# Two transformer layers on one core: the split of a later group's raw weights comes one call of the background work behind their load

## The chip, the cores and the metric

The kernel runs on one core of a Trainium2 chip, as one launch. The metric is the time of that launch on the device in microseconds (us); smaller is better.

## What is computed

The input x is 2048 rows of 512 numbers. Two blocks, an attention A and a gated MLP B, are applied twice with the same weights: x = x + A(norm(x)), x = x + B(norm(x)), and once more. The reference, cut to what matters here:

```
def _A_ref(x, wqkv, wo):
    ...  # 32 heads of 16; phi(t) = where(t > 0, t + 1, exp(t)) + 1e-6
    kv = jnp.einsum("bhsd,bhse->bhde", pk, v)
    ...
    return (num / den) @ wo

def _B_ref(x, w1, w3, w2):          # x 2048x512, w1 and w3 512x1792, w2 1792x512
    gate = jnp.einsum("bsd,df->bsf", x, w1)
    up = jnp.einsum("bsd,df->bsf", x, w3)
    h = _silu(gate) * up
    return jnp.einsum("bsf,fd->bsd", h, w2)

x = A_x
x = x + _A_ref(_layernorm(x), A_wqkv, A_wo)
x = x + _B_ref(_layernorm(x), B_w1, B_w3, B_w2)
x = x + _A_ref(_layernorm(x), A_wqkv, A_wo)
x = x + _B_ref(_layernorm(x), B_w1, B_w3, B_w2)
```

## The kernel before, in words

**Numbers in two parts.** Every float32 operand of a matmul is split into a float16 high part and a float16 rest. `split_late` does it: ScalarE writes the high part at once (L445), and VectorE's rest (L447) is kept in a list, `owed`, and issued when `settle()` is called. `w2` is split by `split` (L412 and L413).

**The MLP.** Its inner width of 1792 is cut into seven groups of 256 columns (numbers 0 to 6), and the 2048 rows into four chunks. In layer 0 the groups come in three sets, (0,1,2), (3,4) and (5,6); a *pass* is one set with one chunk, so there are 4 x 3 + 4 x 2 + 4 x 2 = 28 turns of one group with one chunk. Within a turn, `mlp_group` makes the products in seven parts (a Strassen-like scheme, P1 to P7, twelve matmuls each, L523) into PSUM banks called ba, bb and bc. ScalarE copies a bank out or applies the silu (L1341, L1296), VectorE adds and multiplies (L1344, L1297), four sums (L1312 to L1315, on VectorE or GpSimd) and one more split (L1300 on ScalarE, L1302 on VectorE) make the hidden values, and `mlp_out` (L1388, or L1408 in the plain form) multiplies them by w2 into banks called po. L1437 to L1458 add the result to x.

**The weights.** SBUF holds four slots for split w1/w3 groups. Groups 0 to 2 are prepared during the attention. For groups 4, 3, 5 and 6, in this order, `background` does it during the MLP: `load_raw(g)` issues eight transfers (L547) of 128 KB each into one staging area, the first four for w1 and the last four for w3; `w13_group` splits for w1 one part (128x2x128) and two parts (128x2x256), then the same for w3, makes four sums (L573 to L579) and splits those (128x2x512). `w2_group` follows with two transfers (L778), its splits and sums (L808). It uses the same staging area, half of it for one group, the other half for the next. A load therefore waits for the last reader of its half.

**Who decides the order.** `background` is a generator. After each turn the kernel calls `steps(more, budget)`, with a budget from the table `HOOKS` (0 to 8 in layer 0), under `later(back)`, which gives what is issued a later place in priority:

```
def steps(generator, budget):
    while budget > 0:
        settle()
        step = next(generator, budget)
        budget -= step
```

So a `yield 1` takes one unit and the same call goes on; a yield of more than is left ends the call. Work that a turn needs and that isn't there yet is forced by `ready_for`, step by step. What is issued this way isn't the final order: in the MLP a scheduler of the tile framework places the instructions on each engine by priority and by its own estimate of when they can run. Each engine then executes its list strictly in that order, and an instruction that waits holds up what stands behind it. All DMAs of this kernel are issued from SyncE's queue (SP), in its list's order.

Of the kernel before, what the change touches and what calls it, by code (L numbers as in the profile page):

```python
# [88 lines left out]
def kernel(  # L89
# [21 lines left out]
    def view(at, dtype, *dims):  # L111
        size = 4 if dtype == F32 else 2
        n = size
        for d in dims:
            n *= d
        ap = arena[:, at // 4 : (at + n) // 4]
        if dtype != F32:
            ap = ap.bitcast(dtype)
        if len(dims) > 1:
            names = "abcdefg"[: len(dims)]  # L120
            ap = ap.rearrange(
                f"p ({' '.join(names)}) -> p {' '.join(names)}",
                **{n: d for n, d in zip(names[1:], dims[1:])},
            )
        return ap
# [313 lines left out]
    def settle():  # L439
        while owed:  # L440
            owed.pop(0)()
# [98 lines left out]
    def load_raw(g):  # L540

        dst = view(AT_RAW, F32, 2, 2, 2, 2, P)
        for w, name in enumerate(("w1", "w3")):
            for c in range(2):
                for h in range(2):
                    at = h * (F // 2) + g * P
                    nc.sync.dma_start(dst[:, w, :, c, h], w_rows[name][:, c, :, at : at + P])  # L547

    def w13_group(g, dst):

        if g > 2:
            raw = view(AT_RAW, F32, 2, 2, 4, P)
            quads = [raw[:, :, :, i] for i in range(4)]
            rows = [(w, raw[:, w, :, 2:4], ((0, raw[:, w]),)) for w in range(2)]
        else:
            cols = [slice(h * (F // 2) + g * P, h * (F // 2) + g * P + P) for h in range(2)]
            quads = [st_w13[:, :, c, :, cols[h]] for c in range(2) for h in range(2)]
            both = [
                [
                    st_w13[:, w, c].rearrange("p k (h n) -> p k h n", h=2)[:, :, :, cols[0]]  # L560
                    for c in range(2)
                ]
                for w in range(2)
            ]
            rows = [(w, both[w][1], ((0, both[w][0]), (2, both[w][1]))) for w in range(2)]
        a11, a21, a12, a22 = quads
        scale = [info[n][2] for n in ("w1", "w3")]
        for w, pair, _ in rows:
            split_late(dst[:, w, 0, :, 0], dst[:, w, 1, :, 0], a11[:, w], scale[w])
            yield heavy[0]  # L570
            split_late(dst[:, w, 0, :, 1:3], dst[:, w, 1, :, 1:3], pair, scale[w])
            yield heavy[0]
        engine_of("w13", g).tensor_tensor(a22, a21, a22, OP.add)  # L573
        yield 1
        engine_of("w13", g).tensor_tensor(a21, a11, a21, OP.subtract)
        yield 1
        engine_of("w13", g).tensor_tensor(a11, a22, a11, OP.subtract)
        yield 1
        engine_of("w13", g).tensor_tensor(a12, a12, a11, OP.subtract)  # L579
        yield 1  # L580
        for w, _, parts in rows:
            for i, src in parts:
                n = src.shape[2]
                to = [dst[:, w, part, :, 3 + i : 3 + i + n] for part in range(2)]
                split_late(to[0], to[1], src, scale[w])
                yield heavy[0] * n / 2
# [167 lines left out]
    def store(what, g, src):  # L754
        to = {"w13": w13_d, "w2": w2_d}[what]
        with in_order("SP"):
            nc.sync.dma_start(to[:, g], src)
# [23 lines left out]
    def w2_group(g):  # L781


        raw = w2_raw(g)
        dst, scale = w2_s[g], info["w2"][2]
        yield 1
        split(dst[:, 0, 0], dst[:, 1, 0], raw[:, 0], scale)
        yield 1
        split(dst[:, 0, 1:3], dst[:, 1, 1:3], raw[:, 2:4], scale)
        yield 1  # L790
        later_plain = any(g in gs and plain_run(1, 4 * i + c) for i, gs in enumerate(SETS[1]) for c in range(NC))
        if later_plain or g in w2_a21 and state["plain"]:

            to = w2_a21.get(g, dst[:, :, 6])
            split(to[:, 0], to[:, 1], raw[:, 1], scale)
            if later_plain:
                with in_order("SP"):
                    nc.sync.dma_start(a21_d[:, g], to)
            have.add(("plain", g))
            yield 1  # L800
        a11, a21, a12, a22 = (raw[:, i] for i in range(4))
        for to, a, b, op in (
            (a22, a21, a22, OP.add),
            (a21, a11, a21, OP.subtract),
            (a11, a22, a11, OP.subtract),
            (a12, a12, a11, OP.subtract),
        ):
            engine_of("w2", g).tensor_tensor(to, a, b, op)  # L808
        yield 1
        split(dst[:, 0, 3:], dst[:, 1, 3:], raw, scale)  # L810
        yield 2
        have.add(("w2", g))

    def background(first):

        for tasks in first[::-1]:
            yield from tasks.rest()
        a, b, c = SETS[0]
        for g in a:
            yield from w2_group(g)  # L820
            store("w2", g, view(AT_W2 + SLOT2[g] * GROUP2, F16, GROUP2 // 2))
        late = view(AT_W + 3 * GROUP, F16, 2, 2, 2, 7, P)
        for g in b[::-1]:
            load_raw(g)
            if g == b[-1]:
                for i in a:
                    store("w13", i, view(AT_W + i * GROUP, F16, GROUP // 2))
            yield 1
            yield from w13_group(g, late)
            if g == b[-1]:  # L830
                store("w13", g, view(AT_W + 3 * GROUP, F16, GROUP // 2))
            settle()
            have.add(("w13", g))
            while state["plain"]:
                yield 100
            yield from w2_group(g)
        while state["set"] < 1:
            yield 100
        for g in c:
            load_raw(g)  # L840
            yield 1
            yield from w13_group(g, w13[g])
            settle()
            have.add(("w13", g))
            yield from w2_group(g)
# [628 lines left out]

    def mlp(layer, prep):
        more = background(prep) if layer == 0 else iter(())

        def ready_for(what, g):
# [271 lines left out]
```

## Time and profile before

| | us |
|---|---|
| median of 3 runs | 1174.78 |
| lowest and highest of them | 1173.83, 1175.29 |
| time of the profiled execution | 1172.7 |
| its span, first to last instruction of the trace | 1170.9 |
| TensorE busy in that span | 1147.1 |

The span is what the trace shows of the profiled execution; 1.8 us of its time lie around it. A matmul counts as busy from its start to its modelled end. In rows of the trace, "idle before" is the time that the engine stood still ahead of a row, and the name behind the arrow is what ended that.

### The profile page before, as it was taken

How to read it: one execution, taken by the hardware profiler on the slowest of the kernel's cores; microseconds unless marked ns; L12 is line 12 of the kernel's file. 1: busy time of each engine (PE TensorE's matmuls, PEld its weight loads, DVE VectorE, ACT ScalarE, POOL GpSimd, SP SyncE). 2: the span in 40 equal slices, each digit the busy share in tenths (PEclk: the TensorE clock that was granted, in tenths of full speed). 3: DMA queues.
4: the chain of work that ended last, by engine and by line, in shares of the span. 5: the costliest groups of instructions: out<-in, count | busy, mean ns of one | idle time of the engine just before them, and what ended most of it. 6: DMA issues, size and time to landing. Idle time of an engine off the chain costs nothing.

```text
span 1170.9 us, 21807 instructions
## 1 busy us (share of the span) xinstructions
PE 1147.1 (98%) x8862; PEld 863.5 (74%) x8862; DVE 832.0 (71%) x1401; ACT 638.3 (55%) x1078; POOL 402.8 (34%) x472
## 2 busy tenths in 40 slices
PE   8999998999999999999999999998999999999998
PEld 3445444788888888888864454477888888888887
DVE  6798889977977897778674568757856675656533
ACT  6677787856544554444456644766444344443422
POOL 4343588321000222113368715771252110303120
PEclk9999999999999999999999999999999999999999
DMA  9977565979632221112217425654351351111011
GB/s 279 323 235 233 122 172 119 279 257 278 155 129 100 83 81 64 64 64 73 73 41 209 122 84 116 130 144 125 86 140 64 127 189 48 50 67 37 1 37 37
DMA packets 163396, 147.43 MB, mean 126 GB/s; under 512 B 129632, under 2 KB 138976, under 8 KB 158688
## 3 DMA queue, kind: packets, MB, share of 16 engines
q1 hardware_dynamic: 163296, 146.04, 43.2%
q8 instruction: 69, 1.13, 0.4%
q14 instruction: 31, 0.25, 0.1%
HBM read 72.48 MB, written 42.07 MB: 98 GB/s over the span
## 4 chain that ended last, share of the span: by engine, by line
PE 73%; DVE 8%; DMA 6%; ACT 5%; POOL 4%; issue 2%; SPq 1%; POOLq 0%; DVEq 0%; ACTq 0%
PE bb L523 19%; PE po L1388 16%; PE bc L523 10%; PE pk L523 6%; PE gt L523 6%; PE pq L523 5%; PE po L523 5%; PE ba L523 4%; DMA arena<-arena 3%; DMA arena<-in_B_w_dram 3%; PE po L1408 2%; POOL arena L1283 1%; DVE arena L447 1%; DVE arena L1283 1%; DVE arena L1437 1%
## 5 line engine op out<-in xcount | busy, mean ns | idle before, releaser
L523 PEld LDWEIGHTS <-arena 128*128 128x128 f16 x6360 | 618.3, 98 | 251.3 <-issue 11.6
L523 PE MATMUL bb<-arena 128*128 128x256 f16 x2688 | 330.6, 273 | 4.8 <-DMA arena<-arena 2.3
L1388 PE MATMUL po<-arena 128*128 128x256 f16 x1932 | 234.8, 273 | 6.2 <-ACT arena L1300 3.2
L1388 PEld LDWEIGHTS <-arena 128*128 128x128 f16 x1932 | 188.3, 98 | 30.7 <-ACT arena L1300 5.0
L1341 ACT ACTIVATE arena<-bb 128x512 f32<-128x512 f32 x196 | 114.9, 588 | 132.7 <-PE bb L523 99.3
L523 PE MATMUL bc<-arena 128*128 128x256 f16 x1344 | 165.9, 273 | 0.3 <-DVE arena L1344 0.2
L1302 DVE TENSOR_TENSOR arena<-arena 128x512 f16<-128x512 f32 (+1 forms) x90 | 104.4, 1160 | 81.1 <-ACT arena L1300 80.9
L1300 ACT ACTIVATE arena<-arena 128x512 f16<-128x512 f32 x112 | 99.8, 891 | 104.9 <-DVE arena L1297 47.2
L1296 ACT ACTIVATE arena<-arena,scalars 128x512 f32<-128x512 f32 x112 | 74.7, 667 | 120.9 <-DVE arena L1344 119.9
L1297 DVE SCALAR_TENSOR_TENSOR arena<-arena,scalars 128x512 f32<-128x512 f32 x112 | 86.0, 768 | 50.8 <-ACT arena L1296 50.7
L1344 DVE TENSOR_TENSOR arena<-arena,bc 128x512 f32<-128x512 f32 x112 | 76.4, 682 | 57.7 <-ACT arena L1341 42.3
L1302 POOL TENSOR_TENSOR arena<-arena 128x512 f16<-128x512 f32 x22 | 25.5, 1157 | 230.9 <-ACT arena L1300 206.8
L1457 POOL TENSOR_TENSOR arena<-arena 128x512 f32<-128x512 f32 x25 | 35.7, 1428 | 195.7 <-DVE arena L1437 186.1
L1437 DVE SCALAR_TENSOR_TENSOR arena<-po,scalars,arena 128x256 f32<-128x256 f32 (+1 forms) x170 | 91.9, 584 | 6.5 <-PE po L1388 6.2
L523 PE MATMUL po<-arena 128*128 128x512 f16 x384 | 87.8, 379 | 2.1 <-DMA arena<-arena 2.0
L523 PE MATMUL ba<-arena 128*128 128x256 f16 x672 | 88.7, 274 | 0.0
L523 PE MATMUL gt<-arena 128*128 128x512 f16 x384 | 87.6, 379 | 0.6 <-ACT arena L953 0.3
L523 PE MATMUL pk<-arena 128*128 128x512 f16 x384 | 87.7, 379 | 0.0
L523 PE MATMUL pq<-arena 128*128 128x512 f16 x384 | 87.6, 379 | 0.1
L500 ACT ACTIVATE arena<-arena,nb_all,rs_all 128x512 f32<-128x512 f32 x64 | 50.2, 806 | 23.9 <-POOL nb_all L497 21.0
L1408 PE MATMUL po<-arena 128*128 128x256 f16 x480 | 57.0, 273 | 1.8 <-ACT arena L1300 1.8
L447 DVE SCALAR_TENSOR_TENSOR arena<-arena,scalars 128x512 f16<-128x512 f32 (+2 forms) x60 | 50.1, 856 | 7.9 <-ACT arena L445 6.5
(163 smaller groups left out, 1265.2 us busy)
## 6 DMA issues: line engine op xcount, KB each, us to landing
arena<-xb_d SPq DMA_DIRECT2D x12, 1792.0 KB, 6.8
xb_d<-arena SPq DMA_DIRECT2D x8, 1792.0 KB, 6.5
xt_d<-arena SPq DMA_DIRECT2D x32, 256.0 KB, 2.8
arena<-xt_d SPq DMA_DIRECT2D x32, 256.0 KB, 3.0
arena<-in_B_w_dram SPq DMA_DIRECT2D x8, 896.0 KB, 6.5
arena<-in_B_w_dram SPq DMA_DIRECT2D x28, 256.0 KB, 4.1
w_d<-arena SPq DMA_DIRECT2D x4, 1792.0 KB, 10.3
arena<-w_d SPq DMA_DIRECT2D x4, 1792.0 KB, 6.9
```

What stands on the lines that cost most here:

```text
L447: lambda: nc.vector.scalar_tensor_tensor(lo, src, scale, hi, OP.mult, OP.subtract)
L500: nc.scalar.activation(dst, x_sb[:, t, :], AF.Identity, scale=rs_all[:, t : t + 1], bias=nb_all[:, t : t + 1],)
L523: nc.tensor.matmul(dst, lhs(a, k), rhs(b, k), start=first and k == 0 and i == 0, stop=last and k == n - 1 and i == len(PASSES) - 1, skip_g ...
L1296: nc.scalar.activation(t, gate, AF.Silu, scale=info["u1"])
L1297: nc.vector.scalar_tensor_tensor(t, up, info["hid"], t, OP.mult, OP.mult)
L1300: nc.scalar.activation(hs[:, 0, lo:hi], t[:, lo:hi], AF.Copy)
L1302: engine.tensor_tensor(hs[:, 1, lo:hi], t[:, lo:hi], hs[:, 0, lo:hi], OP.subtract)
L1341: nc.scalar.activation(dst, bank_, AF.Copy)
L1344: nc.vector.tensor_tensor(dst, dst, bank_, OP.add)
L1388: nc.tensor.matmul(po[:, i * HALF : (i + 1) * HALF], hs[:, a, qx, cs], w2[:, b, qw, :], start=g == ends[0] and i + a + b == 0, stop=g == e ...
L1408: nc.tensor.matmul(acc[n][:, half * HALF : (half + 1) * HALF], hs[:, a, qx, cs], w2_a21[g][:, b] if (i, half) == (0, 1) else w2[:, b, i + ...
L1437: nc.vector.scalar_tensor_tensor(dst, src, cb, to, OP.mult, OP.add)
```

## The change

In `background`, the step behind `load_raw(g)` gives back 9 instead of 1, at both places (groups 4 and 3, and groups 5 and 6). Since no budget is above 8, the call in which a load is issued always ends there, and the first split of that group comes in a later call.

```
             if g == b[-1]:
                 for i in a:
                     store("w13", i, view(AT_W + i * GROUP, F16, GROUP // 2))
-            yield 1
+            yield 9
             yield from w13_group(g, late)
...
         for g in c:
             load_raw(g)
-            yield 1
+            yield 9
             yield from w13_group(g, w13[g])
             settle()
             have.add(("w13", g))
```

What the calls issue moves for three groups: group 4's first three splits from the call behind the fifth turn to the one behind the sixth; group 5's first four splits and its sums from the call behind turn 13 to those behind turns 15 and 16; and group 6's whole load from the call behind turn 20 into the forced steps ahead of its own first use, turn 22. (Group 3's load already ended its call.) Most of that vanishes in the scheduler: but for numbers in buffer names, the lists of all engines are the same up to the place where group 6 is loaded, and again from about 60 us later to the end, and GpSimd's list is the same throughout. No instruction is added or taken away.

On SyncE (all DMAs; L547 group 6's raw w1 and w3, L778 group 5's raw w2, L1462 the rows of the next chunk), at the place where group 6 is loaded, one piece of the difference:

```order
 L1462 DMA arena<-xb_d 128x7168
 L766 DMA arena<-w_d 128x7168
-L547 DMA arena<-in_B_w_dram 128x2x128 x3
-L778 DMA arena<-in_B_w_dram 128x512
-L1462 DMA arena<-xb_d 128x7168
-L778 DMA arena<-in_B_w_dram 128x512
+L547 DMA arena<-in_B_w_dram 128x2x128 x4
+L1462 DMA arena<-xb_d 128x7168
+L778 DMA arena<-in_B_w_dram 128x512 x2
+L547 DMA arena<-in_B_w_dram 128x2x128 x3
+L1462 DMA arena<-xb_d 128x7168
 L547 DMA arena<-in_B_w_dram 128x2x128
```

The fourth w1 transfer of group 6 stood behind two w2 transfers and a load of rows; now it follows the third at once. Three of the four w3 transfers now stand ahead of the next load of rows.

On ScalarE at the same place in the program, before (the second row is the split of group 6's first w1 part, L445):

```order
L1296 ACTIVATE arena<-arena,scalars 128x512
L445 ACTIVATE arena<-arena,scalars 128x2x128
L1296 ACTIVATE arena<-bb,scalars 128x256
L1300 ACTIVATE arena<-arena 128x512
L1341 ACTIVATE arena<-bb 128x512
L1296 ACTIVATE arena<-arena,scalars 128x256
L1341 ACTIVATE arena<-bb 128x512
L1300 ACTIVATE arena<-arena 128x1280
L445 ACTIVATE arena<-arena,scalars 128x2x256
```

And with the change:

```order
L1296 ACTIVATE arena<-arena,scalars 128x512
L445 ACTIVATE arena<-arena,scalars 128x2x128
L1296 ACTIVATE arena<-bb,scalars 128x256
L445 ACTIVATE arena<-arena,scalars 128x2x256
L1300 ACTIVATE arena<-arena 128x512
L1341 ACTIVATE arena<-bb 128x512
L1296 ACTIVATE arena<-arena,scalars 128x256
L1341 ACTIVATE arena<-bb 128x512
L1300 ACTIVATE arena<-arena 128x1280
```

The split of the other two w1 parts (128x2x256), which reads the third and fourth transfer, has moved ahead of five instructions of the current turn. Its rest on VectorE (L447) moves with it, ahead of that turn's L1302, L1344 and L1297. Some 30 us on, ScalarE's split of the first w3 part (128x2x128) moves the same way, ahead of the L1296 (128x256), the L1341 and the L1300 (128x1280) that stood in front of it.

On TensorE, at the matmuls that read what that L1300 writes (po, L1388; bb_3950 belongs to the turn in hand, bb_4087 to the next), before:

```order
L523 MATMUL bc_3951<-arena_66 128x256
L1388 LDWEIGHTS arena_66
L1388 MATMUL po0_3877<-arena_66 128x256
L1388 LDWEIGHTS arena_66
L1388 MATMUL po0_3877<-arena_66 128x256
L523 LDWEIGHTS arena_66
L523 MATMUL bb_3950<-arena_66 128x256
```

And with the change:

```order
L523 MATMUL bc_3951<-arena_66 128x256
L1388 LDWEIGHTS arena_66
L1388 MATMUL po0_3877<-arena_66 128x256
L1388 LDWEIGHTS arena_66
L1388 MATMUL po0_3877<-arena_66 128x256
L523 LDWEIGHTS arena_66
L523 MATMUL bb_4087<-arena_66 128x256
```

The two po matmuls keep their place. Behind them, the twelve matmuls of the turn in hand and the first twelve of the next turn (bb_4096 before) have changed places; then the lists agree again for some 10 us.

## Rows read from the trace of the kernel before

**Rows 1.** The page: span, TensorE's busy time, shares of the ending chain.

```profile
span 1170.9 us, 21807 instructions
PE 1147.1 (98%) x8862; PEld 863.5 (74%) x8862; DVE 832.0 (71%) x1401; ACT 638.3 (55%) x1078; POOL 402.8 (34%) x472
...
PE 73%; DVE 8%; DMA 6%; ACT 5%; POOL 4%; issue 2%; SPq 1%; POOLq 0%; DVEq 0%; ACTq 0%
```

**Rows 2.** Busy times by window, summed over 360 to 490 us.

```profile
sum 130.00, PE 129.77 PEld 115.42 DVE 105.59 ACT 63.23 POOL 31.39; mean PE 21.63 PEld 19.24 DVE 17.60 ACT 10.54 POOL 5.23
```

**Rows 3.** Timeline of SyncE's queue: start, duration, line, transfer, count.

```profile
365.06 1.41 SPq L547 DMA_DIRECT2D arena<-in_B_w_dram  x3
366.52 0.46 SPq L778 DMA_DIRECT2D arena<-in_B_w_dram  x1
...
369.12 0.43 SPq L547 DMA_DIRECT2D arena<-in_B_w_dram  x1
395.55 0.33 SPq L1462 DMA_DIRECT2D arena<-xb_d  x1
396.05 2.52 SPq L547 DMA_DIRECT2D arena<-in_B_w_dram  x4
```

**Rows 4.** Issue to landing of L547's three transfers issued from 365.06 us.

```profile
DMA to landing us min/median/max: 2.2/2.3/4.0
```

**Rows 5.** The same for L547's four transfers issued at 318 to 321 us.

```profile
DMA to landing us min/median/max: 2.2/2.4/2.6
```

**Rows 6.** The same for L778's transfer issued at 366.52 us.

```profile
DMA to landing us min/median/max: 4.1/4.1/4.1
```

**Rows 7.** The same for L547's four transfers issued from 396.05 us.

```profile
DMA to landing us min/median/max: 6.1/6.4/6.9
```

**Rows 8.** Timeline of ScalarE: start, duration, instruction, idle before and what ended it.

```profile
368.33 0.63 ACT L1300 ACTIVATE arena<-arena 128x512 f16<-128x512 f32 x1
...
374.28 1.27 ACT L1300 ACTIVATE arena<-arena 128x1280 f16<-128x1280 f32 x1 [1.71 <-POOL arena L1315]
375.98 0.72 ACT L445 ACTIVATE arena<-arena,scalars 128x512 f16<-128x512 f32 x1 [0.43 <-DMA arena<-in_B_w_dram]
...
398.85 0.51 ACT L1296 ACTIVATE arena<-arena,scalars 128x256 f32<-128x256 f32 x1 [2.81 <-DVE arena L1344]
...
402.98 0.51 ACT L445 ACTIVATE arena<-arena,scalars 128x256 f16<-128x256 f32 x1 [0.21 <-DMA arena<-in_B_w_dram]
```

**Rows 9.** Timeline of VectorE, as above.

```profile
369.60 0.68 DVE L1302 TENSOR_TENSOR arena<-arena 128x512 f16<-128x512 f32 x1
370.19 0.68 DVE L1344 TENSOR_TENSOR arena<-arena,ba 128x512 f32<-128x512 f32 x1
370.79 0.48 DVE L1297 SCALAR_TENSOR_TENSOR arena<-arena,scalars 128x256 f32<-128x256 f32 x1
...
377.00 0.74 DVE L447 SCALAR_TENSOR_TENSOR arena<-arena,scalars 128x512 f16<-128x512 f32 x1
```

**Rows 10.** Timeline of GpSimd: the first of the turn's four sums.

```profile
371.35 0.72 POOL L1312 TENSOR_TENSOR arena<-arena 128x256 f32<-128x256 f32 x1 [32.59 <-DVE arena L1297]
```

**Rows 11.** Timeline of TensorE, merged where line and bank agree.

```profile
370.25 0.38 PE L1388 MATMUL po<-arena 128*128 128x256 f16 x2
370.47 2.78 PE L523 MATMUL bb<-arena 128*128 128x256 f16 x24
...
375.71 1.58 PE L1388 MATMUL po<-arena 128*128 128x256 f16 x13
```

**Rows 12.** Timeline of TensorE: when it first reads group 6's weights (slot 2).

```profile
485.87 1.80 PE L523 MATMUL bb<-arena 128*128 128x256 f16 x15
```

**Rows 13.** Timeline of TensorE: two of its longer waits.

```profile
194.86 1.44 PE L523 MATMUL bb<-arena 128*128 128x256 f16 x6 [2.29 <-DMA arena<-arena]
...
312.10 1.47 PE L523 MATMUL bb<-arena 128*128 128x256 f16 x12 [1.60 <-ACT arena L1341]
```

**Rows 14.** Busy times by window, 194 to 198 us (granted clock, DMA share, GB/s last).

```profile
194.00:198.00 4.00, 3.14 (x15) 2.16 (x15) 3.27 (x8) 1.98 (x3) 4.00 (x5) 0.59 0.61 136
```

More of the change, by code (lines that the diff above doesn't have):

```diff
@@ L827, in background @@
                     store("w13", i, view(AT_W + i * GROUP, F16, GROUP // 2))
-            yield 1
+            yield 9
             yield from w13_group(g, late)
@@ L840, in background @@
             load_raw(g)
-            yield 1
+            yield 9
             yield from w13_group(g, w13[g])
```

## The prediction

> **What bounds the kernel now.** I read the page first. TensorE is busy for 1147.1 of 1170.9 us and carries 73% of the chain that ended last [rows 1]; every engine's work that can be seen there hangs on its products. The listing of the change says where to look: all lists are the same up to the load of group 6's raw weights, at 365 us of the trace, and again from about 425 us on. So the change is worth what TensorE's standing time in this stretch becomes. The busy times by window show what there is to gain: from 360 to 490 us TensorE stands for 130.00 - 129.77 = 0.23 us in all [rows 2]. Nothing in this stretch can make the kernel more than 0.23 us faster. What follows the stretch is the same order as before and is fed by TensorE, so a time that TensorE loses here stays lost to the end; I found nothing timed from elsewhere that would absorb it.
>
> Nor is there need for haste with group 6: TensorE first reads its slot at 485.87 us [rows 12], and the split of its w3 parts begins at 402.98 us [rows 8]. The loads and splits are early by tens of us, before and after. What matters is only which instructions of the current turn they stand in front of.
>
> **The change part by part.**
>
> *Groups 4, 3 and 5.* Their splits are issued later by the kernel's code but stand at the same place in every engine's list. Cost and gain are nothing, and no cover is needed for it.
>
> *The fourth w1 transfer.* Now it is issued at 369.12 us, behind two w2 transfers and a load of rows; with the change it takes the place of the w2 transfer at 366.52 us [rows 3]. That is 2.6 us earlier. The two w2 transfers and the rows move back by one place, about 0.5 us; the rows are for the next chunk, and the w2 parts are split behind this turn's instructions on ScalarE, so that costs nothing.
>
> *The split of the second and third w1 part on ScalarE* (128x2x256, which the timeline shows as 128x512). It reads the third and fourth transfer. Before, it began at 375.98 us after 0.43 us of waiting for the fourth, with nothing urgent behind it [rows 8]. With the change it stands in front of the L1300 that began at 368.33 us. Call X the time at which the fourth transfer has landed. ScalarE waits until X. The split takes 0.72 us, and the next instruction starts some 0.09 us before it ends, so L1300 runs from X + 0.63 to X + 1.26 (0.63 us long).
>
> *First wait of TensorE.* Two po matmuls read that L1300. They ran at 370.25 us without a wait [rows 11], since L1300 ended at 368.96. Now they start at X + 1.26 + 0.05 (about what a semaphore took in neighbouring rows) = X + 1.31. Lost: X - 368.94.
>
> *Second wait of TensorE.* VectorE's rest of the split (0.74 us) moves along. It starts 0.05 us behind ScalarE's, at X + 0.77, and with steps of 0.66, 0.59 and 0.60 us [rows 9] L1302, L1344 and L1297 start at X + 1.43, X + 2.02 and X + 2.62; L1297 (0.48 us) ends at X + 3.10. GpSimd's four sums start 0.08 us behind it, as 371.35 follows 370.79 + 0.48 [rows 9, 10]. From their start to that of ScalarE's L1300 (128x1280) are 374.28 - 371.35 = 2.93 us, and that takes 1.27 us [rows 8, 10]. TensorE's next 13 po matmuls, which ran at 375.71 us without a wait [rows 11], can then start at X + 3.10 + 0.08 + 2.93 + 1.27 + 0.05 = X + 7.43. TensorE itself, which needs 375.71 - 370.25 = 5.46 us from the first place to the second, would be there at X + 1.31 + 5.46 = X + 6.77. Lost again: 0.66 us. The two sets of twelve bb matmuls that changed places keep TensorE busy between (2 x 1.31 us), so the delayed L1341 that the turn's own twelve wait for is hidden: it ends near X + 1.8, and they are not reached before X + 2.8. Together the two waits are X + 7.43 - 375.71 = X - 368.28, if X is above 368.94.
>
> *What X is.* Of the three w1 transfers before, issued from 365.06 on about 0.47 us apart, two landed after 2.2 and 2.3 us and the third, issued at 366.0, after 4.0, at 370.0 [rows 3, 4]. The transfer issued at 366.52, in the place that the fourth now gets, landed after 4.1, at 370.66; it has twice the bytes [rows 6]. Four undisturbed ones take 2.2 to 2.6 us [rows 5]. So X lies between 366.52 + 2.6 = 369.1 and 370.7. I take 370.4, since what held up the third then will mostly do so again, and half of the bytes makes it a little earlier than 370.66. That gives 1.46 + 0.66 = **2.1 us** lost; the bounds of X give 0.8 and 2.4.
>
> The Trainium skill, in "DMA: Bandwidth & Descriptors", Queues, rings and completion order, says that a completion count lands only behind every earlier write of the same DMA engine. By that rule X can't be before the third transfer's landing, so with 370.0 for it the loss would be at least 1.7 us and the lower bound of 0.8 falls; by the undisturbed four of [rows 5] it stands. The landings here are in order of issue, which agrees but doesn't prove it.
>
> *The w3 transfers and their split.* The first three now stand in front of a load of rows at 395.55 [rows 3]; behind it, the four landed after 6.1 to 6.9 us [rows 7]. Alone in the queue they should take the 2.2 to 2.6 of [rows 5]. Their first split moves in front of an L1296 that began at 398.85 [rows 8], which by now comes 2 us later, about 400.9. Issued near 396.2 and landed near 398.7, the split (0.51 us) is over by 399.3: nothing lost. The cover is gone if the landing takes more than about 4.2 us. The four transfers and their splits before cost TensorE nothing either, so their earlier landing gains nothing.
>
> *Sum.* 2.1 us, less at most 0.1 of TensorE's own small waits near 427 us, that may vanish when it runs late: 2.0 us. The profiled execution of 1172.7 us becomes 1174.7. It lies 2.1 us below the median of the runs shown, 1174.78, so that median becomes **1176.8 us**, 0.17% more. About 0.2% (2.35 us) is what a measurement of this kernel can tell from no change.
>
> **The rivals.**
>
> *The fourth transfer lands undisturbed*, X = 369.1: 0.8 us lost, 1175.6 us. For it: six of the other w1 transfers in [rows 4, 5] took 2.6 us or less. Against it: the load of rows, which is far bigger, follows at once, as it did behind the two late ones.
>
> *Slower by the w3 loads.* If the first w3 transfer still takes 6.9 us as in [rows 7], it lands at 396.2 + 6.9 = 403.1, and the L1296 behind its split comes at 403.5 instead of 400.9. ScalarE is 2.6 us late in that turn, and TensorE, which has no spare time here [rows 2], loses up to 2.5 more: 4.5 in all, 1179.3 us. It decides from a landing of about 4.2 us on. For it: the transfers of [rows 6] were late with less ahead of them. Against it: the load of rows that was ahead is now behind three of the four.
>
> *Slower by TensorE's clock.* From 194 to 198 us the granted clock was 0.59 of full speed on the mean, so partly the lower of its two levels (1.2 against 2.4 GHz), in a stretch with a wait of 2.29 us [rows 13, 14]. Six bb matmuls took 1.44 us there, about what twelve took at 312.10. After a wait of 1.60 us at 312.10 the clock stayed at full speed [rows 13]. Two waits of 1.5 and 0.7 us are nearer to the second. If it did fall as there, it would take (1 - 0.59) x 4 = 1.6 us more: 1178.4 us. The Trainium skill, "TensorE: Matmul & The Clock Gate", Part 1, says that the clock falls to half after an idle stretch, which agrees with [rows 14].
>
> *Faster.* This would take time off outside the 0.23 us of [rows 2]. No list differs there, so only the change of alignment of DMAs and instruction loads is left. At most a few tenths that I can name, no 0.2%.
>
> *The change does nothing:* true for groups 4, 3 and 5 by the lists, but not for group 6.
>
> **How the numbers follow.** Main case, X from 369.9 to 370.7, 1.6 to 2.4 us slower: 0.55. Undisturbed fourth transfer: 0.13. w3 loads late, or X later than 370.75: 0.20. The clock: 0.07. Faster for a reason that I can't name: 0.05. The main case lies just below the 0.2% line, so of its 0.55 I put 0.07 above it. Slower by over 0.2%: 0.07 + 0.20 + 0.07 = 0.34. Faster by over 0.2%: 0.03, the rest of that case being too small to tell. The same: 0.63. The range goes from 1174.7, just under the undisturbed case, to 1179.3, the late w3 loads; the faster case and the worst of the others, under 2 in 10, are outside.
>
> **What would show it.** In the new trace, ScalarE's split of 128x512 (L445) should start near 370.4 us with about 2 us of idle time ended by a DMA, and TensorE's two po matmuls near 370.25 should show an idle time of about 1.5 us ended by ScalarE's L1300; the 13 po matmuls some 5.5 us on, about 0.7 us, ended by the second L1300. From there to 425 us TensorE should stand for less than 0.3 us. The first w3 split should wait for its transfer without any wait of TensorE near 400 us. If the first two waits are missing, X was earlier than 369; if TensorE waits near 405 us, the w3 loads were late; if TensorE stands elsewhere, or the loss is given back later, the claim that the stretch alone decides is wrong.

## The result, and the profile after

| | before | after |
|---|---|---|
| median of 20 runs, us | 1174.44 | 1178.1 |
| lowest and highest, us | 1173.39, 1178.09 | 1175.76, 1180.51 |
| span of the profiled execution, us | 1170.9 | 1174.1 |

The changed kernel is slower: its time over that of before is 1.0026, 95% interval 1.0018 to 1.0034, which is 3.05 us (2.1 to 4.0) of 1174.44. The forecast was 2.0 us more, 0.17%; 0.26% lies inside the range, but beyond the 0.2% that a measurement can tell. That case had a chance of 0.34; no change clear of 0.2% had been given 0.63.

First the page:

```profile
span 1174.1 us, 21803 instructions
PE 1146.3 (98%) x8862; PEld 862.8 (73%) x8862; DVE 833.5 (71%) x1401; ACT 638.3 (54%) x1078; POOL 403.5 (34%) x472
```

TensorE has the same work as in [rows 1] in a span 3.2 us longer. Busy times by window, summed over 360 to 490 us, say where:

```profile
sum 130.00, PE 127.03 PEld 112.34 DVE 105.33 ACT 61.43 POOL 29.55; mean PE 21.17 PEld 18.72 DVE 17.56 ACT 10.24 POOL 4.92
```

TensorE now stands for 2.97 us of the stretch in which it stood for 0.23 [rows 2]. Its timeline has the places:

```profile
368.71 1.47 PE L523 MATMUL bc<-arena 128*128 128x256 f16 x12
371.71 0.39 PE L1388 MATMUL po<-arena 128*128 128x256 f16 x2 [1.53 <-ACT arena L1300]
...
377.85 1.59 PE L1388 MATMUL po<-arena 128*128 128x256 f16 x13 [0.51 <-ACT arena L1300]
...
428.87 0.49 PE L1388 MATMUL po<-arena 128*128 128x256 f16 x3 [0.38 <-DVE arena L1437]
429.60 0.39 PE L1388 MATMUL po<-arena 128*128 128x256 f16 x2 [0.24 <-ACT arena L1300]
430.08 1.14 PE L523 MATMUL bb<-arena 128*128 128x256 f16 x9
```

The first two waits are the two of the prediction, the two near 429 us are not in it. An idle time understates a loss, since the modelled end of a matmul lies up to 0.2 us behind the start of the next where nothing waits. So losses are read below from starts of the same matmuls in both traces. Three marks serve: **m1**, the twelve bc matmuls ahead of the first wait (368.94 us before, 368.71 after, so 0.23 early); **m2**, the 13 po matmuls (375.71 in [rows 11], now 377.85, 2.15 late unrounded); **m3**, twelve bb matmuls (427.01 before, now 430.08, 3.07 late). Before, m1 and m3:

```profile
368.94 1.47 PE L523 MATMUL bc<-arena 128*128 128x256 f16 x12
...
424.07 2.86 PE L1388 MATMUL po<-arena 128*128 128x256 f16 x23
427.01 1.47 PE L523 MATMUL bb<-arena 128*128 128x256 f16 x12
```

From m1 to m2 2.38 us are lost, from m2 to m3 0.92, together 3.30. From m3 to the end the lag stays at 2.9 to 3.2. By starts, TensorE lost time near 427 us before the change too: twelve matmuls take 1.31 us where nothing waits (370.25 - 368.94), so 23 take 2.51, and they took 427.01 - 424.07 = 2.94, of which the modelled ends show 0.1.

SyncE's queue at the two places:

```profile
364.83 1.92 SPq L547 DMA_DIRECT2D arena<-in_B_w_dram  x4
...
397.21 2.28 SPq L547 DMA_DIRECT2D arena<-in_B_w_dram  x3
399.59 0.42 SPq L1462 DMA_DIRECT2D arena<-xb_d  x1
400.05 0.43 SPq L547 DMA_DIRECT2D arena<-in_B_w_dram  x1
```

The four w1 transfers from 364.83 us on, issue to landing:

```profile
DMA to landing us min/median/max: 2.2/3.2/4.3
```

By the records of the trace the third, issued at 365.78, landed at 370.04, and the fourth, issued at 366.29, at 370.39. The fourth w3 transfer, issued at 400.05 behind the rows:

```profile
DMA to landing us min/median/max: 7.2/7.2/7.2
```

ScalarE (first the split of the w1 parts 2 and 3, then that of the w3 parts 2 and 3, then the last split of group 6's w2):

```profile
370.41 0.72 ACT L445 ACTIVATE arena<-arena,scalars 128x512 f16<-128x512 f32 x1 [2.45 <-DMA arena<-in_B_w_dram]
...
407.24 0.72 ACT L445 ACTIVATE arena<-arena,scalars 128x512 f16<-128x512 f32 x1 [1.14 <-DMA arena<-in_B_w_dram]
...
427.51 1.15 ACT L412 ACTIVATE arena<-arena,scalars 128x1024 f16<-128x1024 f32 x1 [2.62 <-POOL arena L808]
...
428.93 0.62 ACT L1300 ACTIVATE arena<-arena 128x512 f16<-128x512 f32 x1
```

VectorE's rest of the same w3 split, and GpSimd behind it:

```profile
407.99 0.75 DVE L447 SCALAR_TENSOR_TENSOR arena<-arena,scalars 128x512 f16<-128x512 f32 x1 [0.37 <-ACT arena L445]
```

```profile
408.88 1.27 POOL L573 TENSOR_TENSOR arena<-arena 128x512 f32<-128x512 f32 x1 [16.23 <-DVE arena L447]
...
423.20 4.28 POOL L808 TENSOR_TENSOR arena<-arena 128x256 f32<-128x256 f32 x4 [7.49 <-DVE arena L413]
```

Before, the same rows of ScalarE, VectorE and GpSimd:

```profile
404.14 0.72 ACT L445 ACTIVATE arena<-arena,scalars 128x512 f16<-128x512 f32 x1 [0.66 <-DMA arena<-in_B_w_dram]
...
424.45 1.15 ACT L412 ACTIVATE arena<-arena,scalars 128x1024 f16<-128x1024 f32 x1 [2.61 <-POOL arena L808]
```

```profile
404.90 0.75 DVE L447 SCALAR_TENSOR_TENSOR arena<-arena,scalars 128x512 f16<-128x512 f32 x1 [0.21 <-ACT arena L445]
```

```profile
405.79 1.27 POOL L573 TENSOR_TENSOR arena<-arena 128x512 f32<-128x512 f32 x1 [12.30 <-DVE arena L447]
...
420.14 4.28 POOL L808 TENSOR_TENSOR arena<-arena 128x256 f32<-128x256 f32 x4 [7.52 <-DVE arena L413]
```

Read backwards, this is the third wait: TensorE waits for an L1300, which stands behind ScalarE's L412, which waits for GpSimd's sums (L808). They follow group 6's own sums (L573 to L579) through the splits of those, the next w2 transfers and the splits of them, and the sums start when VectorE has done this L447. The part of the wait that an L1437 ended hangs on the same transfers: VectorE's split of them (L413, 128x512) stands ahead of it in its list and began at 422.31, 3.06 us later than before. All five rows are 3.06 to 3.10 us later than before, while TensorE at m2 was only 2.15 late. Before there was no slack in this chain either, since TensorE waited at m3 already.

### The profile page after: what moved, and what is told of

The parts are those of the page before. It is cut to its first block, busy times and chain, and to the rows that moved or that the text cites. A ratio compares the mean times of both kernels' runs of the same rounds, so it can differ in the third digit from the quotient of the medians.

```text
span 1174.1 us, 21803 instructions
## 1 busy us (share of the span) xinstructions
PE 1146.3 (98%) x8862; PEld 862.8 (73%) x8862; DVE 833.5 (71%) x1401; ACT 638.3 (54%) x1078; POOL 403.5 (34%) x472
## 4 chain that ended last, share of the span: by engine, by line
PE 72%; DVE 8%; DMA 6%; ACT 5%; POOL 5%; issue 2%; SPq 1%; POOLq 0%; DVEq 0%; ACTq 0%
PE bb L523 19%; PE po L1388 16%; PE bc L523 10%; PE pk L523 6%; PE gt L523 5%; PE pq L523 5%; PE po L523 5%; PE ba L523 4%; DMA arena<-arena 3%; DMA arena<-in_B_w_dram 3%; PE po L1408 2%; POOL arena L1283 1%; DVE arena L447 1%; DVE arena L1437 1%; DVE arena L1283 1%
## 5 line engine op out<-in xcount | busy, mean ns | idle before, releaser
L1388 PE MATMUL po<-arena 128*128 128x256 f16 x1932 | 234.9, 273 | 8.9 <-ACT arena L1300 5.3
L1388 PEld LDWEIGHTS <-arena 128*128 128x128 f16 x1932 | 188.1, 98 | 34.2 <-ACT arena L1300 7.7
L1341 ACT ACTIVATE arena<-bb 128x512 f32<-128x512 f32 x196 | 115.0, 589 | 133.9 <-PE bb L523 99.5
L1302 DVE TENSOR_TENSOR arena<-arena 128x512 f16<-128x512 f32 (+1 forms) x90 | 104.4, 1159 | 81.5 <-ACT arena L1300 81.3
L1300 ACT ACTIVATE arena<-arena 128x512 f16<-128x512 f32 x112 | 99.8, 891 | 107.6 <-DVE arena L1297 48.0
L1296 ACT ACTIVATE arena<-arena,scalars 128x512 f32<-128x512 f32 x112 | 74.6, 666 | 117.5 <-DVE arena L1344 116.5
L1297 DVE SCALAR_TENSOR_TENSOR arena<-arena,scalars 128x512 f32<-128x512 f32 x112 | 86.3, 770 | 51.6 <-ACT arena L1296 51.5
L1344 DVE TENSOR_TENSOR arena<-arena,bc 128x512 f32<-128x512 f32 x112 | 76.3, 682 | 57.6 <-ACT arena L1341 42.4
L1302 POOL TENSOR_TENSOR arena<-arena 128x512 f16<-128x512 f32 x22 | 25.5, 1160 | 230.8 <-ACT arena L1300 206.7
L1437 DVE SCALAR_TENSOR_TENSOR arena<-po,scalars,arena 128x256 f32<-128x256 f32 (+1 forms) x170 | 91.7, 583 | 5.5 <-PE po L1388 5.2
L447 DVE SCALAR_TENSOR_TENSOR arena<-arena,scalars 128x512 f16<-128x512 f32 (+2 forms) x60 | 49.9, 854 | 9.8 <-ACT arena L445 8.5
```

The source lines that it names most:

```text
L447: lambda: nc.vector.scalar_tensor_tensor(lo, src, scale, hi, OP.mult, OP.subtract)
L1296: nc.scalar.activation(t, gate, AF.Silu, scale=info["u1"])
L1297: nc.vector.scalar_tensor_tensor(t, up, info["hid"], t, OP.mult, OP.mult)
L1300: nc.scalar.activation(hs[:, 0, lo:hi], t[:, lo:hi], AF.Copy)
L1302: engine.tensor_tensor(hs[:, 1, lo:hi], t[:, lo:hi], hs[:, 0, lo:hi], OP.subtract)
L1341: nc.scalar.activation(dst, bank_, AF.Copy)
```

## The experiments

Theory A at this point: three waits, two from ScalarE's split that moved ahead, one from the fourth w3 transfer behind the load of rows. Rivals: an echo (B), the transfers or matmuls that moved (C), the w3 chain alone (D).

In each run, the lists of all engines were held exactly as in the kernel named, but for the rows shown; the order of everything else is fixed by issue-order dependencies. No run leaves out or changes part of the computation, but the last adds matmuls. The ratio is to the kernel before, measured beside it. "L447 late" is the start of VectorE's split of the w3 parts 2 and 3 against 404.90 before, less the lag at m2.

| run | ratio (95%) | m1 to m2, us | m2 to m3, us | L447 late, us |
|---|---|---|---|---|
| the change | 1.0026 (1.0018 to 1.0034) | 2.38 | 0.92 | 0.94 |
| e1_pairback | 1.0005 (0.9996 to 1.0014) | 0.00 | 1.56 | 1.57 |
| e2_w3first | 1.0022 (1.0012 to 1.0032) | 1.92 | 0.55 | 0.49 |
| e3_both | 1.0001 (0.9992 to 1.0009) | 0.00 | 0.90 | 0.73 |
| e4_splitonly | 1.0079 (1.0067 to 1.0091) | 8.92 | 0.05 | -0.04 |
| e5_w2back | 0.9994 (0.9984 to 1.0004) | 0.00 | -0.04 | -0.05 |
| e6_earlysplit | 1.0018 (1.0008 to 1.0028) | 2.24 | 0.04 | -0.05 |
| e7_sponly | 1.0010 (1.0001 to 1.0018) | 0.00 | 0.89 | 0.88 |
| e8_rowslate | 1.0034 (1.0021 to 1.0047) | 2.10 | 1.21 | 1.14 |
| e9_fetch | 1.0037 (1.0023 to 1.0051) | 0.77 | 0.78 | 0.75 |

But for e9_fetch, which adds work elsewhere, each interval holds the ratio that the two losses give (the change: 1 + 3.30 / 1174.4 = 1.0028). Outside m1 to m3 the lags of single executions wander by up to 3.3 us with equal lists, which is why they are measured between marks. Each loss is of one execution; those of e1_pairback and e3_both lie near the upper ends of their intervals (1.0013 and 1.0008), so other executions may have lost less.

**e1_pairback.** From the changed kernel; ScalarE, and VectorE likewise with its L447, L1302, L1344, L1297:

```
-L445 ACTIVATE arena<-arena,scalars 128x2x256
 L1300 ACTIVATE arena<-arena 128x512
 L1341 ACTIVATE arena<-bb 128x512
 L1296 ACTIVATE arena<-arena,scalars 128x256
 L1341 ACTIVATE arena<-bb 128x512
 L1300 ACTIVATE arena<-arena 128x1280
+L445 ACTIVATE arena<-arena,scalars 128x2x256
```

> The changed kernel with every engine's list held as it is, but the split of group 6's w1 parts 2 and 3 (ScalarE's L445 and VectorE's L447, 128x2x256) put back behind that turn's L1300 and L1302 (128x1280). The early fourth w1 transfer, the exchanged bb matmuls and the order of the w3 loads stay. Theory A, three waits of separate causes (two from this split standing in front, 1.5 and 0.5 us; one from the fourth w3 transfer behind the load of rows, 1.0 us): the waits near 371 and 377 us are gone, the one near 427 us stays, about 1.0 us over the kernel before, ratio to it 1.0009. Theory B, the wait near 427 is only an echo of the first two: nothing is left, 1.0000. Theory C, the early transfer or the exchanged matmuls cost the time: all stays, 1.0026. Theory D, the w3 loads alone set the whole delay at 427 us, whatever came before: the first two waits go, but TensorE waits about 3 us near 427 us, 1.0026.

The first two waits are gone, with the early transfer and the exchanged matmuls still there: theory C fell. Theory B fell too, as 1.56 us are lost near 427 us, and so did D, which had about 3 us there. ScalarE:

```profile
407.14 0.72 ACT L445 ACTIVATE arena<-arena,scalars 128x512 f16<-128x512 f32 x1 [1.52 <-DMA arena<-in_B_w_dram]
```

The third loss is 0.64 us larger than in the change, and larger than A expected. The fourth w3 transfer was issued at 399.10, 0.95 us earlier than in the changed kernel, but took 8.01 us instead of 7.16 and landed at 407.11, about when it did there (407.21), though TensorE was 0.73 us less late at m2. Why it took longer in this execution isn't shown.

**e2_w3first.** From the changed kernel, SyncE:

```
 L547 DMA arena<-in_B_w_dram 128x2x128 x3
+L547 DMA arena<-in_B_w_dram 128x2x128
 L1462 DMA arena<-xb_d 128x7168
-L547 DMA arena<-in_B_w_dram 128x2x128
```

> The changed kernel with every list held, but on SyncE's queue the load of rows that stood in front of the fourth w3 transfer of group 6 now stands behind it. A: the waits near 371 and 377 us stay (1.5 and 0.5 us), the transfer lands about 2.5 us after its issue instead of 7.2, the wait near 427 us is gone: about 2.1 us over the kernel before, ratio 1.0017. B: if the third wait is an echo of the first two, it stays, 3.1 us, 1.0026. C: the early w1 transfer or the exchanged matmuls; nothing changes near 371, and this run tells nothing more of it. D: 2.1 us, as A.

The fourth w3 transfer landed 3.0 us after its issue, at 402.70, 4.5 us earlier than in the changed kernel, and ScalarE's split of it didn't wait. But the third loss shrank only to 0.55 us. The late landing alone doesn't make it: my theory A was wrong here, and so was D. VectorE:

```profile
406.32 1.49 DVE L1302 TENSOR_TENSOR arena<-arena 128x1280 f16<-128x1280 f32 x1 [1.34 <-ACT arena L1300]
407.73 0.75 DVE L447 SCALAR_TENSOR_TENSOR arena<-arena,scalars 128x512 f16<-128x512 f32 x1
```

L447 follows L1302 without a wait: here VectorE's own list holds it up.

**e3_both.** Both edits.

> The two edits before together: the split of the w1 parts 2 and 3 put back behind the turn's L1300, and the fourth w3 transfer in front of the load of rows. All else of the change stays: the early fourth w1 transfer, the exchanged bb matmuls, the first w3 split in front of three instructions of its turn. A, and B: no wait over 0.3 us from 365 to 432 us, the time of the kernel before, ratio 1.0000, at most 0.2 us off. C: still 2 to 3 us over it, 1.0017 to 1.0026. D: 1.0000.

By the time alone this run would have confirmed A; the trace says otherwise. 0.90 us are still lost near 427 us. VectorE:

```profile
395.16 1.28 DVE L413 SCALAR_TENSOR_TENSOR arena<-arena,scalars 128x1024 f16<-128x1024 f32 x1 [0.70 <-ACT arena L412]
...
405.39 1.49 DVE L1302 TENSOR_TENSOR arena<-arena 128x1280 f16<-128x1280 f32 x1 [1.34 <-ACT arena L1300]
406.80 0.75 DVE L447 SCALAR_TENSOR_TENSOR arena<-arena,scalars 128x512 f16<-128x512 f32 x1
```

Again L447 follows L1302 without a wait. VectorE's list differs from before in a place that the prediction passed over: the last w2 split of group 5 (L412 on ScalarE, L413 on VectorE, 128x1024) moved ahead of an L1437, an L1297 and another L1437. VectorE stands 0.70 us for it, nearly all of the 0.73 by which L447 is late, and what it had done before by then comes after.

**e4_splitonly.** From the kernel before, the converse of the diff of e1_pairback; the fourth transfer keeps its late place.

> The kernel before with every list held, but the split of the w1 parts 2 and 3 (L445 and L447, 128x2x256) put in front of the turn's L1300 and L1302 (128x512), as the change has it, while the fourth w1 transfer keeps its late place, where it landed at 375.96 us. A: ScalarE waits some 8 us, TensorE about 375.96 - 368.94 = 7.0 us near 371 us and some 0.7 us more about 6 us later: 7.7 us, ratio 1.0065; nothing is lost near 427 us beyond that, since the w3 loads stand as before. B: as A. C: no more than 0.3 us, since neither the transfers nor the matmuls have moved: 1.0000. If less than 7 us is lost, TensorE has other work there that the prediction's sum left out.

The fourth transfer landed at 376.25. TensorE and the granted clock (window columns: stretch, length, busy times, clock behind POOL's):

```profile
377.57 0.61 PE L1388 MATMUL po<-arena 128*128 128x256 f16 x2 [6.73 <-ACT arena L1300]
378.05 4.55 PE L523 MATMUL bb<-arena 128*128 128x256 f16 x24
```

```profile
377.50:381.50 4.00, 3.93 (x19) 2.75 (x20) 1.88 (x4) 1.49 (x4) 1.97 (x3) 0.50 0.00 0
```

The first wait costs 6.89 us (7.32 late there, 0.43 at m1); the sum's X - 368.94, against a TensorE that was itself 0.43 late, gives 6.88. Then the granted clock is 0.50, its lower level, for 4 us, and from the start of the two po matmuls to the end of the 24 bb it takes 4.87 us instead of 2.84 (starts of what follows: 382.44 here, 373.09 before): 2.0 us more, in which the second wait of 0.66 vanishes. Theory A's 7.7 us became 8.92. The clock rival is real, but not at the change's 1.5 us: there the granted clock was 1.00 in each window from 360 to 490 us.

**e5_w2back.** From e3_both; ScalarE, then VectorE:

```
+L1439 ACTIVATE arena<-po_4212,scalars 128x256
+L1296 ACTIVATE arena<-arena,scalars 128x512
 L412 ACTIVATE arena<-arena,scalars 128x1024
-L1439 ACTIVATE arena<-po_4212,scalars 128x256
-L1296 ACTIVATE arena<-arena,scalars 128x512
...
+L1437 SCALAR_TENSOR_TENSOR arena<-po_4212,scalars,arena 128x256
+L1297 SCALAR_TENSOR_TENSOR arena<-arena,scalars 128x512
+L1437 SCALAR_TENSOR_TENSOR arena<-po_4213,scalars,arena 128x256
 L413 SCALAR_TENSOR_TENSOR arena<-arena,scalars 128x1024
-L1437 SCALAR_TENSOR_TENSOR arena<-po_4212,scalars,arena 128x256
-L1297 SCALAR_TENSOR_TENSOR arena<-arena,scalars 128x512
-L1437 SCALAR_TENSOR_TENSOR arena<-po_4213,scalars,arena 128x256
```

> Run e3_both, and besides the split of the last w2 part of group 5 (128x1024: ScalarE's L412, VectorE's L413) put back: on ScalarE behind that turn's L1439 and L1296 (128x512), on VectorE behind an L1437, the L1297 (128x512) and a second L1437, about as before. In e3_both TensorE still waited near 428 us for 0.38 and 0.24 us, and VectorE stood 0.70 us for this split at 395 us. Theory E: the third wait is set by the later of two chains, the fourth w3 transfer's landing and VectorE's turn, which starts late because this split moved ahead in its list; with both undone no wait over 0.3 us is left near 427 us, and from 365 to 432 us TensorE loses under 0.3 us. Theory F, it is the exchange of the matmuls or the later order of the lists as a whole: the 0.9 us lost there in e3_both stays. By the time alone, 1.0000 or a little below e3_both's 1.0001.

Nothing is lost from m1 to m3. TensorE runs through the place near 427 us, and VectorE's split didn't wait (this execution was 3.3 us late already at m1):

```profile
427.27 2.93 PE L1388 MATMUL po<-arena 128*128 128x256 f16 x23
430.29 1.47 PE L523 MATMUL bb<-arena 128*128 128x256 f16 x12
```

```profile
397.99 1.27 DVE L413 SCALAR_TENSOR_TENSOR arena<-arena,scalars 128x1024 f16<-128x1024 f32 x1
...
408.17 0.75 DVE L447 SCALAR_TENSOR_TENSOR arena<-arena,scalars 128x512 f16<-128x512 f32 x1
```

Theory E holds, F fell: the exchanged matmuls and all other differences of the lists cost nothing in this execution. The split was put back on both engines at once, so which of the two lists matters is not separated.

**e6_earlysplit.** From the kernel before: the diff of the split as in e4_splitonly, and SyncE's first place as in the change.

> The kernel before with every list held, but the two edits at 366 us made as in the change: the fourth w1 transfer directly behind the third on SyncE, and the split of the w1 parts 2 and 3 (L445 and L447, 128x2x256) in front of the turn's L1300 and L1302 (128x512). No matmul is exchanged, and nothing else of the change is there. Theory E (and A of the first runs): waits of 1.5 us near 371 us and 0.5 to 0.7 us near 377 us, none beyond 0.2 us near 427 us: 2.1 us, ratio 1.0018. Theory F, if all lists together matter, and the exchange of the matmuls hides something: more than 2.4 us. If the third wait is an echo of the first two after all: 3.1 us, 1.0026.

```profile
371.67 0.39 PE L1388 MATMUL po<-arena 128*128 128x256 f16 x2 [1.39 <-ACT arena L1300]
...
377.82 1.59 PE L1388 MATMUL po<-arena 128*128 128x256 f16 x13 [0.26 <-ACT arena L1300]
```

2.24 us and nothing beyond, 1.0018, as E had it. This is the change that the prediction had in mind; the third loss is apart from it.

**e7_sponly.** From the kernel before, SyncE's order of the change alone (the diff stands in the section on the change).

> The kernel before with ScalarE, VectorE, GpSimd and TensorE held, and only SyncE's queue in the order of the change: the fourth w1 transfer early, and the load of rows between the third and the fourth w3 transfer instead of in front of the four. Theory E: no wait near 371 us; the fourth w3 transfer is issued near 398.6 and lands some 7.2 us later, near 405.7 instead of 404.1 us, and as nothing in that chain has slack, TensorE waits some 1.4 us near 427 us: ratio 1.0012. If the landing of that transfer has slack in the order of before, less; by theory F nothing, 1.0000.

```profile
405.62 0.72 ACT L445 ACTIVATE arena<-arena,scalars 128x512 f16<-128x512 f32 x1 [1.97 <-DMA arena<-in_B_w_dram]
```

```profile
427.29 0.49 PE L1388 MATMUL po<-arena 128*128 128x256 f16 x3 [0.61 <-DVE arena L1437]
```

The landing, 405.60, was as expected, but 0.89 us are lost instead of 1.4: this execution was 0.60 us late at m2 already. The issue follows that lag (398.49 here and 400.05 in the changed kernel, each 397.9 without its lag at m2), so the expected 398.6, for a kernel that isn't late, was 0.7 us too late. So either cause alone costs up to 0.9 us at m3: the late fourth w3 transfer (here 0.89), or VectorE's list (0.90 in e3_both, 0.55 in e2_w3first). The later of the two sets it: the last two columns of the table agree within 0.17 us in all ten rows.

**e8_rowslate.** From the changed kernel, SyncE:

```
-L1462 DMA arena<-xb_d 128x7168
 L778 DMA arena<-in_B_w_dram 128x512 x2
+L1462 DMA arena<-xb_d 128x7168
```

> The changed kernel with every list held, but the load of rows at 366.8 us (1.8 MB) moved behind the two w2 transfers that follow it. It asks what made the third and fourth w1 transfer take 4.1 to 4.3 us. G1, that load of rows, issued 0.5 us behind the fourth: both land 2.2 to 2.6 us after their issue, the fourth by 368.9, the first wait falls to 0.1 and the second to 0.5 us at most: 1.6 us over before with the third wait, ratio 1.0013. G2, what else is on the queues then (the transfers themselves, the w2 transfers, an instruction packet): the fourth still takes about 4 us, and the ratio stays 1.0026.

The second to the fourth w1 transfer, issue to landing:

```profile
DMA to landing us min/median/max: 2.7/3.8/4.0
```

The third and fourth were as late as ever, with the rows issued 2.6 us behind the fourth: G1 fell. The ratio didn't fall either. In all ten traces so far one packet on the instruction queue (q8) lies among these transfers, and the third landed 1.28 to 1.38 us behind its end.

**e9_fetch.** From the changed kernel:

```
                 keep_busy(10)
+                for _ in range(40):
+                    nc.tensor.matmul(warm[:, :P], ones16, ones16, start=True, stop=True)
```

> The changed kernel with every list held, but 40 small matmuls (128x128) of the same constants added among the warm-up matmuls at the kernel's start, that no result depends on. In all ten traces so far one packet of instructions (16 KB, 0.9 to 1.6 us, on one of the DMA engines) falls among the w1 transfers at 367 to 371 us, and the third transfer landed 1.3 us behind the end of this packet, whatever it took from its issue (3.8 to 4.5 us). Such packets come every 14 us here, about 128 matmuls; 40 more matmuls at the start make this one come some 4.4 us earlier against the transfers, so before the first of them. G3, the packet made the third and fourth transfer late: all four land 2.2 to 2.7 us after their issue, the fourth by about 368.9; the first wait is under 0.2 us and the second about 0.6. The third wait, near 427 us, is set by the late fourth w3 transfer as in e1_pairback, and grows to 1.0 to 1.7: in all 1.6 to 2.3 us lost from 365 to 432 us instead of 3.3, ratio 1.0012 to 1.0020, and up to 1 us more for the added matmuls at the start. If the packet is only there by chance: the third and fourth still take about 4 us, and 3.3 us are lost.

The four w1 transfers, and what TensorE still waits for:

```profile
DMA to landing us min/median/max: 2.2/2.6/2.7
```

```profile
381.45 1.59 PE L1388 MATMUL po<-arena 128*128 128x256 f16 x13 [0.50 <-ACT arena L1300]
```

The packet now began at 367.53, 2.5 us ahead of the first transfer; the fourth landed 2.50 us after its issue, and the first wait is gone. G3 holds, in this one execution. The third loss, expected at 1.0 to 1.7 us, came at 0.78, so from m1 to m3 1.55 us are lost, just under the expected 1.6 to 2.3. The time itself rose: the added matmuls delay the start by over 2 us, more than I had allowed, and this execution lost more elsewhere, so the ratio tells nothing here.

## Why the prediction was right, and where not

**The first two waits were right to a few hundredths.** The sum had the po matmuls at X + 1.31 and the 13 po at X + 7.43, with X the fourth landing. With the landings measured: the change 370.39 gives 371.70 and 377.82, measured 371.71 and 377.85; e6_earlysplit 370.36 gives 371.67 and 377.79, measured 371.67 and 377.82; e8_rowslate 372.11 gives 373.42 and 379.54, measured 373.43 and 379.56. X was taken as 370.4 and came at 370.39. The reason given for that, that what held up the third transfer would do so again, was right, though the prediction didn't know what it was. The load of rows, which it held against the rival of the undisturbed transfer, was not it (e8_rowslate); the packet was (e9_fetch). That rival's 0.8 us is about what e9_fetch lost from m1 to m2, 0.77. The Trainium skill, "DMA: Bandwidth & Descriptors" (Queues, rings and completion order), says that a completion count lands only behind every earlier write of the same DMA engine. The landings agree: the fourth landed 0.35 to 0.37 us behind the third wherever it was issued next to it.

**The exchanged matmuls, and groups 4, 3 and 5, cost nothing**, as said: e5_w2back has all of that, loses nothing from m1 to m3, and its ratio is 0.9994 (0.9984 to 1.0004).

**The step that failed is "The w3 transfers and their split", costed at nothing; it measured 0.92 us.** It looked at the first w3 transfer only, which landed after 2.6 us, inside the 2.2 to 2.6 taken. The fourth, which now stands alone behind the load of rows, took 7.2, and its split is what the rest of the chain waits for. The premise "the four transfers and their splits cost TensorE nothing either" hid that the chain had no slack to lose: the 0.1 us near 427 us, written off as able to vanish, was its end. By starts it was some 0.4 us, so the 0.23 us that the prediction took for all of TensorE's standing time in the stretch, from modelled ends, was too small. The third loss would have been there by the transfer alone (e7_sponly). It is made inside the stretch in which the lists differ (L447 near 408 us) and shows behind its end at 425 us.

**A second cause was not looked for.** "What matters is only which instructions of the current turn they stand in front of", the prediction says of group 6's loads and splits. Group 5's w2 splits (L412 and L413) moved too, and e3_both and e5_w2back show the price of the last of them, 128x1024 at 393 to 396 us: put back, it takes the 0.90 us away. In the changed kernel the fourth landing is the later of the two causes, by 0.45 us: with e3_both's step of 1.41 us from L1302 to L447, VectorE could have begun L447 at 406.13 + 1.41 = 407.54, and began at 407.99. VectorE there:

```profile
395.91 1.27 DVE L413 SCALAR_TENSOR_TENSOR arena<-arena,scalars 128x1024 f16<-128x1024 f32 x1
...
406.13 1.49 DVE L1302 TENSOR_TENSOR arena<-arena 128x1280 f16<-128x1280 f32 x1 [1.34 <-ACT arena L1300]
```

So VectorE alone would have made L447 0.49 us late, as it did in e2_w3first. But the 128x1024 L413 doesn't wait in these two, and the trace points to something else: the w2 split before it (L413, 128x512) moved ahead of L1313 to L1315, so GpSimd's sums on it (L808) ran beside L1314 and L1315, which took 0.53 us longer each (last section). No run put that row back alone, so this is argued, not shown.

**The rival "slower by the w3 loads"** named the first of these transfers, not the fourth, and its wait near 405 us did not come: the loss shows 22 us after the landing, through GpSimd. That the range reached up to 1179.3, and so held a third loss that the sum had left out, is due to this rival, and in that part luck. **The clock** rival failed at this size. With 0.92 added to the 2.0 the forecast would have been 2.9 us more, inside the measured 2.1 to 4.0.

## What to carry to other kernels

When a change reorders a queue of transfers, follow the last transfer of each group, not the first, to the end of the chain that reads it; a wait at that end, even one that shows as 0.1 us as here, says that the chain has no slack. Compare the lists of every engine over the whole stretch, since a later engine's order can be a second cause as large as the first, and curing one of the two shows little in the time. A split moved ahead in an in-order list costs the landing of its last input, so it is safe only behind that landing.

## What the runs showed of the hardware

**A packet of instructions delays a transfer.** Every 13 to 16 us in this stretch one packet on the instruction queue takes 0.9 to 1.6 us; the queue's row from 367.4 to 368.8 us of the changed kernel (packets, MB, share):

```profile
q8 instruction: 1, 0.02, 5.9%
```

5.9% of 16 engines over 1.4 us is 1.3 us of one engine. The third w1 transfer landed 1.28 to 1.38 us behind the packet's end in ten executions, 3.8 to 4.5 us after its issue; with the packet moved away (one execution), 2.65. The Trainium skill, "Runtime: NRT & Kernel Launch", Instruction fetch mechanics, calls the cost of crossing a 16 KiB boundary "mostly hidden". Here it was hidden in the kernel before, where the third transfer landed as late (4.0 us, [rows 4]) and nothing urgent waited for it. In the changed kernel, where an engine waits for the transfer, it is not: with the packet's delay 2.38 us are lost from m1 to m2, without it 0.77.

**The clock fell after one wait and not after another like it.** Before, TensorE stood 2.29 us and the clock fell [rows 13, 14]. In the changed kernel it stood 2.26 us at the same place, and the window from 194.6 us shows full speed:

```profile
194.60:198.20 3.60, 3.32 (x29) 2.83 (x29) 2.61 (x8) 2.28 (x4) 3.60 (x5) 1.00 0.44 111
```

All eleven traces have this wait. Over the 4 us behind it the granted clock was 0.57 to 0.63 in five of them (before, e1_pairback, e2_w3first, e6_earlysplit, e7_sponly; waits of 2.24 to 2.35 us) and 1.00 in the other six (waits of 2.23 to 2.31 us). So the length of the wait doesn't decide it here; what does stays open. After 6.73 us (e4_splitonly) it fell.

**VectorE's and GpSimd's sums take longer side by side.** In the changed kernel two of VectorE's sums took 0.95 and 0.94 us, where 0.42 is usual, beside GpSimd's four sums:

```profile
389.43 0.95 DVE L1314 TENSOR_TENSOR arena<-arena 128x256 f32<-128x256 f32 x1
390.30 0.94 DVE L1315 TENSOR_TENSOR arena<-arena 128x256 f32<-128x256 f32 x1
```

```profile
389.25 3.39 POOL L808 TENSOR_TENSOR arena<-arena 128x256 f32<-128x256 f32 x4 [12.76 <-DVE arena L413]
```

In e3_both the same four GpSimd sums took 5.15 us instead of 3.39, and VectorE's 0.42 each:

```profile
388.79 5.15 POOL L808 TENSOR_TENSOR arena<-arena 128x256 f32<-128x256 f32 x4 [13.38 <-DVE arena L413]
```

Which of the two pays went with the list: VectorE in the change, e2_w3first, e8_rowslate and e9_fetch (0.95 and 0.94 us each time), where the w1 split stands ahead; GpSimd in e1_pairback, e3_both and e5_w2back (5.15 or 5.16 us), where it was put back. What decides it isn't shown.
